# Second stage of a Fourier transform: two array tiles of 64 rows by 128 columns in place of four of 64 by 64

## The chip, the cores and the metric

The kernel runs on one core of a Trainium2 chip. The metric is the time on the device, in microseconds (us), of one execution: the median of three runs. Besides these, one execution was recorded by the hardware profiler; every duration below that is not called a median comes from that execution. TensorE (PE in the profile) has two levels of clock, 1.2 and 2.4 GHz; the profile calls them a granted clock of 0.5 and 1.0.

## The reference

The input is 8 sequences of 1856 rows with 256 features. A layer of a spectral kind comes first, and a mixture of experts after it:

```python
X = np.fft.rfft(x, axis=1)
Yr = Xr @ w_r - Xi @ w_i + b_r
Yi = Xr @ w_i + Xi @ w_r + b_i
Yr = np.sign(Yr) * np.maximum(np.abs(Yr) - lam, 0.0)     # Yi alike, lam = 0.01
y = np.fft.irfft(Yr + 1j * Yi, n=1856, axis=1)           # then 14848 rows of 256
g_idx = argmax(y @ w_group)                              # one of 4 groups
e_idx = argmax(y @ w_expert[g_idx])                      # one of 4 experts in it
out = g_w * e_w * (relu(y @ w1[g, e]) @ w2[g, e])        # 256 -> 1024 -> 256
```

## The kernel before

The sequences are worked on in four pairs (`pr`, two sequences `bt` in each). 1856 is 58 x 32, so the forward transform has two stages. The first (`a_mm`, line 349) sums over 58 rows with matmuls in four array tiles of 64 x 64; VectorE turns the result in blocks of 32 x 32 (line 353), which leaves, on 64 partitions for each half `h` of the 256 features, the 32 rows and the two parts (cosine, sine) that the second stage sums over. The second stage (`f_mm`, line 675) is the one that changes. For one frequency class (`k`, `kp`) and one sequence `bt` it multiplies the turned data, as the stationary operand, with a table `T` of 64 rows and 64 columns. The two halves `h` of the features lie on partitions 0 to 63 and 64 to 127, and so in different rows of the array; the 128 features of a half are cut again into two times 64 (`dh`), which lie in different columns of the array. Each matmul is of type float32 and leaves two loads of weights and two matmul records in the trace. One call of `f_mm`, a unit, fills the two banks of one PSUM tile with four frequency classes: 64 matmul records (32 where only half a tile is left). There are 30 full units' worth in all, 1920 records.

ScalarE and VectorE take the result out of PSUM (`f_high`, `f_low`, `d_copy`, `d_sub`, lines 692 to 707), and TensorE multiplies it with the complex weights (`m_common`, `m_mm`, lines 739, 742 and 757). The inverse transform has two stages as well (`b_mm`, line 782; `p_mm`, line 801). Its result goes to memory and through the router (`g_mm`, line 834; `route_g`), and GpSimd writes each row's number and weight into the list of its expert with indirect DMAs of 128 rows each (`scatter`, line 254; 128 of them in the kernel). The experts follow (lines 492, 565, 566 and others).

Steps of the four pairs, of the router, of the scatters and of the first expert jobs are interleaved by a string written out by hand (`ORDER`, lines 45 to 61), a letter for a step; `e` is one unit of `f_mm`. The instructions of TensorE, VectorE, ScalarE, SyncE and GpSimd keep the order of this string on their engine. Each scatter also waits for a matmul step that stands before it in the string (`pace`, lines 257 to 260), and for the third scatter before it.

Of the kernel before, what the change touches and what calls it, by code (L numbers as in the profile page):

```python
# [131 lines left out]
def spectral_moe(ctx: ExitStack, tc: tile.TileContext, x, wri, bri, wgate, w1, w2, cst, out):  # L132
    nc = tc.nc
# [178 lines left out]
    T = cf.tile([128, K1, 64], F32, name="T")  # L312
# [7 lines left out]
    def banks():  # L320
        return pa.tile([128, 2, 512], F32, name="bank")
# [15 lines left out]
    zys = {}  # L337
# [280 lines left out]
    def steps_of(*dims):  # L618

        def wrap(fn):  # L620
            def run():
                for idx in np.ndindex(*[len(d) for d in dims]):
                    fn(*[d[i] for d, i in zip(dims, idx)])
                    yield
            return run()
        return wrap
# [38 lines left out]
    @steps_of(pairs, u8)  # L665
    def f_mm(pr, kk):
        psum["f", pr, kk] = unit = banks()
        for k in range(2 * kk, min(2 * kk + 2, 15)):
            c0 = k % 2 * 256
            for kp in range(2):  # L670
                for bt in range(2):
                    m = (2 * kp + bt) * 32
                    for dh in range(2):
                        for h in range(2):
                            nc.tensor.matmul(unit[64 * dh:64 * dh + 64, h, c0:c0 + 256].rearrange("p (j c) -> p j c", j=2)[:, :, m:m + 32],  # L675
                                             lhsT=zys[pr][64 * h:64 * h + 64, k, bt, 64 * dh:64 * dh + 64, kp],
                                             rhs=T[64 * h:64 * h + 64, 2 * k + kp, :], start=True, stop=True, skip_group_check=True)

    def side(ins, what, pr, kk, h):
        apart(ins, (what, pr, kk, h), *((o_, pr, kk, 1 - h) for o_ in ("hs" if what in "fc" else "fc")))  # L680
# [325 lines left out]
    def first_rows(_):  # L1006
# [5 lines left out]

    steps = dict(
        Q=weight_steps(), l=load_steps(), c=a_mm, d=a_turn, e=f_mm, f=f_high, h=f_low, i=d_copy, g=d_sub, j=m_bias, p=c_high, q=c_low, y=m_common, z=m_share, k=m_mm,
        m=m_relu, o=m_shrink, r=b_mm, s=b_turn,
        v=p_mm, w=p_out, x=p_turn,
# [291 lines left out]
    for i, (kind, q) in enumerate(jobs):  # L1308
# [5 lines left out]
        if i + 1 < len(jobs) and jobs[i + 1][0] == "r":  # L1314
            k, part = jobs[i + 1][1]
# [44 lines left out]
    with tc.For_i(KF, nfx, 1) as iv:  # L1360
# [9 lines left out]
        hts, h = [], hq.tile([128, 8, WIDE], F32, name="hh")  # L1370
# [43 lines left out]
```

## Time and profile before

| | |
|---|---|
| time, median of 3 runs (lowest to highest) | 1117.25 us (1115.56 to 1117.4) |
| time of the profiled execution | 1122.26 us |
| its span, from first to last instruction | 1120.5 us |
| mean granted clock of TensorE | 0.972 |
| TensorE matmul busy | 1052.7 us, 94% of the span |
| VectorE, ScalarE, GpSimd busy | 661.4, 488.2 and 429.6 us |
| matmuls of line 675 | 1920 records, 49.2 us busy, 20.7 us idle before them |

The transforms take about the first 345 us, with the first expert jobs starting inside the stretch that follows; the rest is the experts. Busy time of TensorE is the union of its records' durations, and a record lasts longer than it keeps its part of the array, so the busy share says little about how fast matmuls follow each other; for that one looks at how many records start in a stretch. "issue" as the cause of an idle time means that the engine waited for nothing that the profile shows.

### The profile page before, as it was taken

The numbers are of one execution on the slowest core, as the hardware profiler recorded it, in microseconds if no ns is written. First come the engines' busy times: TensorE is split into PE (matmuls) and PEld (weight loads), VectorE is DVE, ScalarE is ACT, GpSimd is POOL, SyncE is SP. The second block draws the span as 40 slices with busy tenths as digits, with TensorE's granted clock in tenths as the row PEclk, the third lists the DMA queues.
The fourth block names the chain that finished last, engine by engine and source line by source line (L and its number), as shares of the span: only waits on it lengthen the run. The fifth ranks groups of instructions, "written<-read, shape, count | busy, mean of one in ns | idle before, by whom it ended". The sixth has DMA issues, their size and how long they took to land.

```text
span 1120.5 us, 24142 instructions
## 1 busy us (share of the span) xinstructions
PE 1052.7 (94%) x9400; PEld 910.5 (81%) x9400; DVE 661.4 (59%) x1574; ACT 488.2 (44%) x1249; POOL 429.6 (38%) x519
## 2 busy tenths in 40 slices
PE   7999989889888888799999999999999999999996
PEld 4886767764665677688999999999999999999996
DVE  6879987664776766336636554536455456455532
ACT  2664545331542444223435553435445345444532
POOL 0120254443434466656234333334335343332422
PEclk9999999896998999899999999999999999999999
DMA  9504402320231453014223233313133133133110
GB/s 380 189 2 149 155 2 101 128 78 2 77 133 39 133 170 77 20 52 134 72 72 133 79 101 104 103 51 128 47 114 130 44 122 117 52 109 113 45 34 28
DMA packets 38886, 106.94 MB, mean 95 GB/s; under 512 B 17596, under 2 KB 19993, under 8 KB 32242
## 3 DMA queue, kind: packets, MB, share of 16 engines
q1 hardware_dynamic: 18130, 57.74, 15.4%
q0 software_dynamic: 15744, 30.71, 8.9%
q10 hardware_dynamic: 4896, 16.93, 3.9%
q8 instruction: 75, 1.23, 0.5%
q14 instruction: 41, 0.34, 0.1%
HBM read 71.26 MB, written 34.23 MB: 94 GB/s over the span
## 4 chain that ended last, share of the span: by engine, by line
PE 56%; issue 4%; DVE 1%; ACT 1%; another core or an unknown queue 1%; POOL 1%; DMA 0%; POOLq 0%; ACTq 0%; DVEq 0%
PE ph L492 24%; PE py L565 12%; PE py L566 6%; PE py L587 6%; PE pg L475 2%; PE ph L925 2%; PE bank L949 1%; PE bank L951 1%; PE py L600 1%; DMA lst<-ent,sloti 0%; PE bank L834 0%; DVE hl L937 0%; POOL out_dram L539 0%; POOL lst L254 0%
## 5 line engine op out<-in xcount | busy, mean ns | idle before, releaser
L492 PE MATMUL ph<-xth,big 128*128 128x256 f32 (+8 forms) x1280 | 290.9, 311 | 2.1 <-DVE rk_o L1146 1.2
L499 DVE SCALAR_TENSOR_TENSOR hl<-ph,hh 128x256 fp32r<-128x256 f32 (+8 forms) x528 | 168.7, 356 | 108.3 <-ACT hh L497 89.3
L492 PEld LDWEIGHTS ph<-xth,big 128*128 128x128 f32 x1280 | 216.5, 188 | 4.9 <-PE ph L492 1.9
L565 PE MATMUL py<-big,hh 128*128 128x512 f32 (+2 forms) x608 | 219.0, 400 | 0.0
L492 PE MATMUL ph<-xtl,big 128*128 128x256 f32 (+8 forms) x640 | 198.1, 310 | 0.3 <-DVE xtl L480 0.3
L497 ACT ACTIVATE hh<-ph 128x256 fp32r<-128x256 f32 (+8 forms) x528 | 153.0, 337 | 99.6 <-PE ph L492 84.9
L457 POOL DMA_INDIRECT xg<-ys_d,gi_r x92 | 90.3, 981 | 244.5 <-PE pg L475 222.7
L254 POOL DMA_INDIRECT lst<-ent,sloti x128 | 128.3, 1003 | 140.4 <-PE pw L757 42.0
L566 PE MATMUL py<-big,hl 128*128 128x256 f32 (+2 forms) x608 | 171.4, 282 | 0.2 <-DVE hl L499 0.2
L565 PEld LDWEIGHTS py<-big,hh 128*128 128x128 f32 (+2 forms) x608 | 113.0, 186 | 27.1 <-DVE yo L606 0.3
L539 POOL DMA_INDIRECT out_dram<-yo,si_r x92 | 92.0, 1000 | 93.3 <-issue 44.7
L492 PEld LDWEIGHTS ph<-xtl,big 128*128 128x128 f32 x640 | 120.3, 188 | 0.7 <-DVE xtl L480 0.5
L566 PEld LDWEIGHTS py<-big,hl 128*128 128x128 f32 (+2 forms) x608 | 113.2, 186 | 1.1 <-DVE hl L499 0.8
L571 DVE SCALAR_TENSOR_TENSOR yo<-py,ent_r,yo 128x256 f32<-128x256 f32 (+1 forms) x66 | 31.9, 484 | 135.2 <-ACT yo L570 119.9
L570 ACT ACTIVATE yo<-py,ent_r 128x256 f32<-128x256 f32 (+1 forms) x66 | 31.4, 475 | 150.6 <-PE py L566 93.7
L587 PE MATMUL py<-hh,big 128*128 128x320 f32 (+4 forms) x320 | 75.3, 315 | 0.0
L723 POOL TENSOR_TENSOR xdl<-xd,xdh 128x512 fp32r<-128x512 f32 (+1 forms) x23 | 28.1, 1223 | 118.3 <-ACT xdh L716 93.7
L757 PE MATMUL pw<-wh,xh 128*128 128x256 f32 x240 | 68.2, 305 | 4.5 <-DVE pw L747 2.3
L439 DVE TENSOR_TENSOR big<-xt,big 128x512 fp32r<-128x512 f32 x104 | 71.1, 684 | 1.0 <-ACT big L438 0.2
L675 PE MATMUL bank<-T,big 64*64 64x64 f32 x1920 | 49.2, 228 | 20.7 <-issue 18.0
L675 PEld LDWEIGHTS bank<-T,big 64*64 64x64 f32 x1920 | 40.5, 137 | 34.3 <-issue 24.6
L438 ACT CAST big<-xt 128x512 fp32r<-128x512 f32 x104 | 65.3, 628 | 0.0
(217 smaller groups left out, 1953.1 us busy)
## 6 DMA issues: line engine op xcount, KB each, us to landing
xt<-in_w_dram SPq DMA_DIRECT2D x34, 1024.0 KB
ys_d<-ysb ACTq DMA_DIRECT2D x32, 512.0 KB
big<-in_x_dram SPq DMA_DIRECT2D x8, 1024.0 KB
xt<-in_x_dram SPq DMA_DIRECT2D x8, 1024.0 KB
lst<-ent,sloti POOLq DMA_INDIRECT x128
lst<-L SPq DMA_DIRECT2D x1, 1920.0 KB
xg<-ys_d,gi_r POOLq DMA_INDIRECT x92
out_dram<-yo,si_r POOLq DMA_INDIRECT x92
```

Source lines behind the costliest of these rows:

```text
L254: ins = nc.gpsimd.indirect_dma_start(out=lst, out_offset=bass.IndirectOffsetOnAxis(ap=sl_, axis=0), in_=en_, in_offset=None, bounds_check= ...
L439: nc.vector.tensor_tensor(out=wt[:, 2 * i + 1, cs], in0=raws[i][:, cs], in1=wt[:, 2 * i, cs].bitcast(F32), op=ALU.subtract)
L457: ins = nc.gpsimd.indirect_dma_start(out=xg[0:m, c, :], out_offset=None, in_=ys_d[0:rows, :], in_offset=bass.IndirectOffsetOnAxis(ap=ids.g ...
L492: nc.tensor.matmul(o[:, :n], lhsT=a_[:, ch, fs], rhs=b_[:, ch, 0:n], start=k == 0, stop=k == 5)
L497: nc.scalar.activation(out=hh[:, f, cs], in_=o[:, cs], func=AF.Relu)
L499: nc.vector.scalar_tensor_tensor(out=hl[:, f, cs], in0=o[:, cs], scalar=0.0, in1=hh[:, f, cs].bitcast(F32), op0=ALU.max, op1=ALU.subtract)
L539: ins = nc.gpsimd.indirect_dma_start(out=out, out_offset=bass.IndirectOffsetOnAxis(ap=ids.si[0:ids.rows(t), t:t + 1], axis=0), in_=ysb, in ...
L565: nc.tensor.matmul(o, lhsT=hh[:, f, ts], rhs=w2b[:, :, f, :], start=f == 0, stop=f == 7, skip_group_check=True)
L566: nc.tensor.matmul(o[:, 0:D], lhsT=hl[:, f, ts], rhs=w2h[:, f, :], start=False, stop=f == 7, skip_group_check=True)
L587: nc.tensor.matmul(o, lhsT=w_[:, f, ds_], rhs=h_[:, f, 0:n], start=f == 0 and h_ is hh and w_ is w2h, stop=f == 7 and h_ is hh and w_ is n ...
L675: nc.tensor.matmul(unit[64 * dh:64 * dh + 64, h, c0:c0 + 256].rearrange("p (j c) -> p j c", j=2)[:, :, m:m + 32], lhsT=zys[pr][64 * h:64 * ...
L757: ins = nc.tensor.matmul(y, lhsT=a_[:, h, k % 2, j], rhs=t[:, j, h], start=False, stop=a_ is xl and h == 1, skip_group_check=True)
```

## The change

The loop over `dh` goes away. One matmul takes all 128 features of a half as its stationary operand, and writes all 128 partitions of the PSUM bank. The two halves `h` stay in different rows of the array, so there are two array tiles of 64 rows by 128 columns instead of four of 64 by 64. The moving operand, the sums, the places of the results and all other steps are as they were.

```diff
                     m = (2 * kp + bt) * 32
-                    for dh in range(2):
-                        for h in range(2):
-                            nc.tensor.matmul(unit[64 * dh:64 * dh + 64, h, c0:c0 + 256].rearrange("p (j c) -> p j c", j=2)[:, :, m:m + 32],
-                                             lhsT=zys[pr][64 * h:64 * h + 64, k, bt, 64 * dh:64 * dh + 64, kp],
-                                             rhs=T[64 * h:64 * h + 64, 2 * k + kp, :], start=True, stop=True, skip_group_check=True)
+                    for h in range(2):
+                        nc.tensor.matmul(unit[:, h, c0:c0 + 256].rearrange("p (j c) -> p j c", j=2)[:, :, m:m + 32],
+                                         lhsT=zys[pr][64 * h:64 * h + 64, k, bt, :, kp],
+                                         rhs=T[64 * h:64 * h + 64, 2 * k + kp, :], start=True, stop=True, skip_group_check=True)
```

On TensorE, at the unit of the second stage that starts at 43.06 us in the trace of before, stands this (`pw` is the product with the complex weights, `bank` a PSUM tile; the last number is how many alike follow each other, and each float32 matmul of line 675 leaves two records):

```order
L757 MATMUL pw<-wl,xh 128x256
L757 MATMUL pw<-wh,xl 128x256 x2
L675 MATMUL bank<-T,big 64x2x32 x32
L349 MATMUL bank<-big,cA 64x512 x4
L739 MATMUL pw<-wch,xdh 128x256
L739 MATMUL pw<-wcl,xdh 128x256
```

And in the changed kernel, where all lines behind the edit have a number that is lower by one:

```order
L756 MATMUL pw<-wl,xh 128x256
L756 MATMUL pw<-wh,xl 128x256 x2
L674 MATMUL bank<-T,big 128x2x32 x16
L349 MATMUL bank<-big,cA 64x512 x4
L738 MATMUL pw<-wch,xdh 128x256
L738 MATMUL pw<-wcl,xdh 128x256
```

The unit keeps its place; it has 16 matmuls on 128 output partitions for 32 on 64. At the unit that starts at 162.85 us, behind a step of the inverse transform (line 782) of the pair before, the same engine has in the kernel before:

```order
L757 MATMUL pw<-wh,xl 128x256 x2
L782 MATMUL bank<-big,CI 64x512 x16
L675 MATMUL bank<-T,big 64x2x32 x32
L739 MATMUL pw<-wch,xdh 128x256
L739 MATMUL pw<-wcl,xdh 128x256
```

And in the changed kernel:

```order
L756 MATMUL pw<-wh,xl 128x256 x2
L781 MATMUL bank<-big,CI 64x512 x16
L674 MATMUL bank<-T,big 128x2x32 x16
L738 MATMUL pw<-wch,xdh 128x256
L738 MATMUL pw<-wcl,xdh 128x256
```

Here too nothing has moved but the count and the shape. The same holds for all 28 places of the line, and the rows of the other four engines are the same in both kernels but for line numbers.

## Rows read from the trace of the kernel before

**Rows 1.** Page, busy time: us, share of the span, instructions.

```profile
PE 1052.7 (94%) x9400; PEld 910.5 (81%) x9400; DVE 661.4 (59%) x1574; ACT 488.2 (44%) x1249; POOL 429.6 (38%) x519
```

**Rows 2.** Windows: length, busy us of each engine (instructions), granted clock, DMA share, GB/s.

```profile
30.00:150.00 120.00, 115.84 (x1899) 91.54 (x1892) 104.97 (x216) 69.26 (x151) 23.54 (x22) 1.00 0.33 109
150.00:345.00 195.00, 170.94 (x2159) 124.36 (x2158) 132.58 (x284) 79.06 (x173) 85.97 (x91) 0.88 0.23 75
```

**Rows 3.** Waits of TensorE, 150 to 345 us: total us, times, longest.

```profile
PE bank L675 <- issue: 16.1, 35, 1.1
```

**Rows 4.** Windows, line 675 alone, each unit of 30 to 150 us: length, PE, PEld.

```profile
35.69:36.67 0.98, 0.98 (x64) 0.98 (x64) 1.00 1.18 359
...
sum 13.59, PE 13.57 PEld 13.58; mean PE 1.04 PEld 1.04
```

**Rows 5.** Windows, line 675 alone, each unit from 150 us on.

```profile
162.85:167.61 4.76, 2.44 (x64) 1.90 (x64) 0.94 0.03 4
177.40:178.32 0.92, 0.92 (x64) 0.92 (x60) 1.00 0.00 0
...
sum 42.15, PE 25.53 PEld 20.26; mean PE 1.82 PEld 1.45
```

**Rows 6.** Timeline of TensorE, 12 to 24 us: start, us, what, records, idle before.

```profile
18.08 0.35 PE L675 MATMUL bank<-T,big 64*64 64x64 f32 x8 [1.41 <-DVE big L353]
18.68 2.02 PE L675 MATMUL bank<-T,big 64*64 64x64 f32 x117 [0.24 <-DVE big L353]
22.55 1.13 PE L675 MATMUL bank<-T,big 64*64 64x64 f32 x60 [1.85 <-issue]
```

**Rows 7.** Line 675, then line 742: duration ns min/median/max, first and last start.

```profile
L675 PEld LDWEIGHTS bank<-T,big x1920: 132/135/226, 16.3 to 333.5; 64*64 64x64 f32 x192
L675 PE MATMUL bank<-T,big x1920: 212/220/367, 16.3 to 333.5; 64*64 64x64 f32 x192
L742 PEld LDWEIGHTS pw<-wc,xd x68: 186/190/337, 24.5 to 347.5; 128*128 128x128 f32 x68
L742 PE MATMUL pw<-wc,xd x68: 378/379/794, 24.5 to 347.8; 128*128 128x256 f32 x68
```

**Rows 8.** Line 223: loads of bfloat16 weights.

```profile
L223 PEld LDWEIGHTS <-ones x8: 95/97/101, 129.8 to 437.6; 128*128 128x128 bf16 x8
```

**Rows 9.** Timeline of TensorE, 162 to 172 us.

```profile
162.85 1.26 PE L675 MATMUL bank<-T,big 64*64 64x64 f32 x43 [0.56 <-DVE big L790]
164.49 0.36 PE L675 MATMUL bank<-T,big 64*64 64x64 f32 x5 [0.39 <-issue]
165.22 0.35 PE L675 MATMUL bank<-T,big 64*64 64x64 f32 x5 [0.37 <-issue]
...
168.22 0.41 PE L739 MATMUL pw<-wcl,xdh 128*128 128x256 f32 x1
168.43 0.41 PE L739 MATMUL pw<-wch,xdh 128*128 128x256 f32 x1
```

**Rows 10.** Timeline of GpSimd, 160 to 169 us.

```profile
163.06 0.97 POOL L254 DMA_INDIRECT lst<-ent,sloti  x1 [0.30 <-issue]
```

**Rows 11.** Timeline of TensorE, 310 to 315 us.

```profile
312.15 0.40 PE L675 MATMUL bank<-T,big 64*64 64x64 f32 x12
313.14 1.08 PE L675 MATMUL bank<-T,big 64*64 64x64 f32 x52 [0.59 <-issue]
```

**Rows 12.** Windows of TensorE alone: length, busy (records), granted clock.

```profile
167.00:170.40 3.40, 3.00 (x18) 0.50 0.01 0
248.90:262.60 13.70, 13.32 (x71) 0.50 0.02 2
...
sum 34.10, PE 32.25; mean PE 5.38
```

**Rows 13.** Waits of GpSimd, 150 to 340 us.

```profile
POOL lst L254 <- PE pw L757: 39.0, 8, 14.0
```

**Rows 14.** Timeline of GpSimd, 300 to 480 us.

```profile
414.40 1.02 POOL L254 DMA_INDIRECT lst<-ent,sloti  x1 [5.48 <-DVE sloti L241]
```

## The prediction

> **What bounds the kernel now.** I read the page first, then windows of all engines, then the waits of TensorE, then line 675 by itself, unit by unit. TensorE is the busiest engine by far, 94% of the span against 59% for the next [rows 1]. The changed line lies in the first 335 us, so I looked there. From 30 to 150 us TensorE is busy for 115.8 of 120 us at the full clock. From 150 to 345 us it is busy for only 170.9 of 195 us, at a mean granted clock of 0.88, while no other engine passes 132.6 us [rows 2]. What makes it idle there is mostly not another engine: 16.1 us, in 35 pieces, stand directly before line 675 with "issue" as their cause [rows 3]. So TensorE bounds both stretches, and in the second one something holds it up at the very line that changes.
>
> The units show it. The 13 rows of units between 30 and 150 us (11 of 64 records, two of 96, so 14 units) take 13.59 us, 0.97 us a unit, without a break [rows 4]. The 14 rows from 150 us on (12 of 64, two of 32, so 13 units) take 42.15 us where 13 x 0.97 = 12.6 us would do [rows 5]: 29.5 us are stalls. They are uneven: one unit takes 0.92 us, another 4.76 us. In the slow one 43 records run in the first 1.26 us, then 5 records come every 0.7 us, and the engine waits for nothing in between [rows 9]. GpSimd is issuing scatters 0.30 us behind each other at that moment [rows 10]. This is so everywhere: the ten unit rows that lie beside such indirect DMAs are those that break, and the 17 others after the first block never do. I take this as the mechanism: while GpSimd issues indirect DMAs, instructions reach TensorE slowly (some ten in 0.7 us), and line 675, whose records start 15 ns apart, uses up what is queued. Nothing in the trace says why they come slowly.
>
> Six of the breaks are followed by a slow clock: six stretches of 34.1 us in all, between 167 and 303.5 us, run at 0.50, each beginning inside or right behind a broken unit [rows 12]. There line 739 starts a record every 0.21 us [rows 9].
>
> The stalls are not made by the profiler: the profiled execution took 1122.26 us, only 5.0 us over the median of 1117.25 us, and stalls and slow clock together are far more. I work out the sum in the profiled execution and carry it to the median as it is.
>
> **The change part by part.** Removed are 960 matmuls and 960 loads; added is width: each remaining load has 128 columns for 64. TensorE's order is otherwise the same and so is every other engine's, so no DMA, wait or queue is passed.
>
> *Longer loads.* Now four tiles share 64 records in 0.97 us, so each tile takes 16 loads, one every 61 ns. After, two tiles share 32 records: again 16 loads in each. A 64-column float32 load lasts 135 ns, a 128-column one 190 ns, and at its shortest 132 and 186: 54 ns more [rows 7]. The load sets the pace if the tile's own matmul is hidden under it; a record of line 742 with 256 columns lasts 379 ns, one of line 675 with 64 lasts 220 ns, so 64 columns keep the tile for about 53 ns (159 ns / 3, an estimate), and 61 ns a pair leaves no room for load and matmul one after the other. So a unit grows by 16 x 54 ns = 0.85 us, to 1.82 us. Bounds: nothing (a tile's pace stays at 61 ns), or twice the time if the two tiles took turns, which the present four do not. I take 0.85 us. Before 150 us: 14 x 0.85 = +11.9 us, with nothing to hide it (TensorE idles 4.2 us of 120, in waits that follow its own order). From 150 us on: 13 x 0.85 = +11.0 us.
>
> *The first block,* three units from 16.33 to 23.5 us, waits 1.41 and 0.24 us for VectorE, which stays, and 1.85 us for "issue" after 117 records [rows 6]. 3 x 0.85 = 2.55 us more, and I take the 1.85 us as gone, with half the instructions: +0.7 us; +2.5 us if not.
>
> *Stalls.* Nine of the ten units that break do so after 26 to 43 records, the tenth after 12 [rows 9, 11]. A unit will have 32, and last long enough (1.82 us) for some 12 more to arrive. So nearly every unit should be through on what is queued. The lines behind start from an emptier queue, so I leave 6 of the 29.5 us: -23.5 us. Bounds: 0 and -29.5 us.
>
> *Clock.* The stretches at 0.50 hold 3.7 us of the broken units themselves; the other 30.4 us would take at best half, -15.2 us. Some of that is work that waits for instructions or DVE at either clock (71 records in 13.7 us is less than the clock explains), so I take two thirds: -10 us. Bounds: 0 and -15.2 us.
>
> Sum: +0.7 + 11.9 + 11.0 - 23.5 - 10 = -9.9 us, 1122.3 to 1112.4 us in the profile, 1117.25 to about 1107 us in the median. With all bounds at their best end but the loads as taken, -21 us: 1096 us.
>
> What is late next: GpSimd. It waits for TensorE for 39.0 us in this stretch at one line alone [rows 13], so it has room to come earlier; a scatter's own place still follows TensorE's steps.
>
> **Two rules weighed.** Line 223 loads 128 columns of bfloat16 in 97 ns, line 742 as many of float32 in 190 ns, and neither has column tiles [rows 7, 8]. The Trainium skill (TensorEngine Tiling (Array Packing), Restrictions and Gotchas) says that column tiling shuts out a fast way of loading weights, which would speak for dropping it; another of its pages (TensorE: Matmul & The Clock Gate, Weight-path perf modes) says that float32 has no such way. The two durations agree with the second page, so the first rule should bring nothing; if it did, the loads would cost nothing, which is the third rival's sum.
>
> The Trainium skill (TensorE: Matmul & The Clock Gate, The mechanism) says that a load overlaps a running matmul only in other rows of the array. By it a tile of the changed kernel would do load and matmul one after the other, the second rival's case. The 61 ns a pair of today, less than a load and a matmul together,, speak against it for loads of 64 columns; no run here shows it for 128.
>
> **Rivals.**
> 1. *Slower: the breaks follow time, not count.* If scatters hold up the instructions from their own start, whatever is queued, a unit of 32 breaks as one of 64 did. For it: one unit broke after 12 records and 0.2 us [rows 11]. Against: 26 to 43 in the others, and units beside no scatter never break. Then the 9.5 broken units stay as long as now, the clock stays, the 1.85 us stay, and the other units pay: 2.5 + 11.9 + 3.5 x 0.85 = +17.4 us, 1135 us. It decides if fewer than about 16 records get through before the first break. Chance 0.18.
> 2. *Slower: load and matmul in turn.* A pair takes 61 + 54 + 53 = 168 ns in place of 115, so 30 x 16 x 53 ns = 25.4 us more than the forecast: 1133 us. Chance 0.06.
> 3. *Faster: the wide load costs nothing.* 30 x 0.85 = 25.5 us less: about 1082 us. No float32 row is that short. Chance 0.06.
> 4. *No change: given back later.* From 414 us GpSimd issues scatters almost without a gap, and what TensorE gained might only lengthen the wait for them. Against: that run of scatters begins after a wait of 5.48 us for the router on VectorE [rows 14], which hangs on TensorE's own steps and would come earlier with them. 1117 us, two to either side. Chance 0.10.
>
> **How the numbers follow.** The forecast has 0.60, with its own range of 1096 to 1115 us. Rivals 1, 2 and 3 lie outside it. From 1090 to 1135 us leaves out rival 3 (0.06) and about half of rival 1 with a little of rival 2, some 0.13. A difference of 0.2%, 2.2 us, is about what a measurement of this kernel can tell from none. Faster by more: the forecast less a little (0.58) and rival 3, 0.64. Within: most of rival 4 and the forecast's upper edge, 0.12. Slower: rivals 1 and 2, 0.24.
>
> **What the changed profile would show.** Units of line 674 before 150 us of about 1.8 us with 32 records, and no break; 1.0 us would show rival 3, 2.7 us rival 2. From 150 us on a sum over the 14 rows of about 30 us (24 without any break) against 42.15; over 40 is rival 1. "issue" before the line down from 16 us to a few. A granted clock from 150 to 345 us of 0.95 or more for 0.88; if the clock stays at 0.88, the term of -10 us is wrong. If all three are as said and the end does not move, it is rival 4, and the gap must stand between 345 and 480 us.

## Result: slower by 0.6%, and the profile after

The changed kernel takes 1124.35 us (median of 20 runs, 1118.72 to 1128.91), the kernel before in the same rounds 1116.42 us (20 runs, 1109.59 to 1123.22). The ratio is 1.0062, with a 95% interval of 1.0044 to 1.0081. The forecast was 1107 us, with a range of its own from 1096 to 1115 us: the kernel was to become some 10 us faster, and by the medians it became 7.9 us slower.

The profiled execution of the changed kernel took 1119.59 us, with a span of 1117.8 us. That is 2.7 us *less* than the span of before. The profiled execution of before (1122.26 us) would lie near the top of its runs, the one of after lies near the bottom of its own. So the two traces can say what each stretch does, but not which kernel is faster; for that the timed runs stand.

The page's busy times, and the two stretches by windows, answer to [rows 1, 2]; the last row is a window of TensorE alone, in the first block (length, busy, records, granted clock):

```profile
PE 1067.2 (95%) x8440; PEld 925.8 (83%) x8440; DVE 662.9 (59%) x1574; ACT 488.1 (44%) x1249; POOL 429.3 (38%) x519
```

```profile
30.00:150.00 120.00, 118.42 (x1324) 93.73 (x1324) 95.88 (x187) 62.18 (x131) 16.75 (x15) 1.00 0.33 108
150.00:345.00 195.00, 181.76 (x1932) 137.25 (x1932) 150.26 (x332) 90.22 (x199) 95.28 (x101) 0.99 0.23 75
```

```profile
20.10:30.30 10.20, 10.20 (x84) 0.50 1.00 414
```

The mean clock from 150 to 345 us is now 0.99 for 0.88. But from 20.1 us, inside the first units of the changed line, TensorE runs at 0.50 for 10.2 us, while its records lie end to end. Before, that stretch was at full clock.

The units of line 674, one row each (length, PE, PEld, clock): the last three before 163.5 us with the sum of those 13 rows, against [rows 4], and some of the 14 later rows with their sum, against [rows 5]:

```profile
147.44:149.28 1.84, 1.84 (x32) 1.84 (x32) 1.00 0.00 0
154.12:156.89 2.77, 2.77 (x48) 2.77 (x48) 1.00 0.00 0
161.63:163.46 1.83, 1.83 (x32) 1.83 (x32) 1.00 0.01 1
sum 25.72, PE 25.71 PEld 25.71; mean PE 1.98 PEld 1.98
...
178.98:180.82 1.84, 1.84 (x32) 1.84 (x32) 1.00 0.02 1
190.99:192.82 1.83, 1.83 (x32) 1.83 (x32) 1.00 0.15 63
208.23:210.06 1.83, 1.83 (x32) 1.83 (x32) 1.00 0.74 287
...
242.40:243.29 0.89, 0.89 (x16) 0.89 (x16) 1.00 0.12 37
...
331.03:331.92 0.89, 0.89 (x16) 0.89 (x16) 1.00 0.03 1
sum 23.77, PE 23.76 PEld 23.76; mean PE 1.70 PEld 1.70
```

Every full unit takes 1.83 us, where 1.82 was forecast, and none breaks: 13.59 us have become 25.72, and 42.15 have become 23.77. The loads and matmuls of the line, against [rows 7] (ns, min/median/max):

```profile
L674 PEld LDWEIGHTS bank<-T,big x960: 189/193/329, 18.1 to 331.9; 64*128 64x128 f32 x192
L674 PE MATMUL bank<-T,big x960: 277/278/419, 18.1 to 331.9; 64*128 64x64 f32 x192
```

A load lasts 193 ns for 135. From one record of a tile to its next pass 118 ns, for 60 before: 58 ns more, as much as a load lasts longer, and not the 168 ns that rival 2 gave for load and matmul in turn. So load and matmul overlap in one tile here too, and the rule that the prediction put beside rival 2, that a load overlaps a matmul only in other rows, does not hold for these loads. The Trainium skill (TensorE: Matmul & The Clock Gate, LDWEIGHTS (loading the stationary operand)) puts a load at its number of columns divided by 1.2, in ns: for 128 columns some 107 ns, an estimate from that formula, and the pace of 118 ns in the trace is near it.

What TensorE waits for from 150 to 345 us, against [rows 3] (us in total, times, longest):

```profile
PE pw L756 <- DVE pw L746: 4.1, 7, 1.5
PE pw L756 <- issue: 3.3, 3, 2.0
PE bank L781 <- issue: 1.3, 3, 0.8
PE bank L833 <- issue: 0.8, 1, 0.8
```

The 16.1 us of "issue" before the changed line are gone. A little of it stands at other lines now. All that the prediction wanted to see in this trace is there: 1.8 us a unit, no break, a sum of 24 us, "issue" gone, the clock at 0.99. Still the timed runs are not faster. So the question is where the gain went.

TensorE from 254 to 264 us in the changed kernel shows it (start, us, records, idle before):

```profile
255.30 2.10 PE L674 MATMUL bank<-T,big 64*128 64x64 f32 x32
257.33 1.13 PE L741 MATMUL pw<-wc,xd 128*128 128x256 f32 x4
258.39 3.07 PE L781 MATMUL bank<-big,CI 32*64 32x512 f32 x30
261.61 0.62 PE L781 MATMUL bank<-big,CI 32*64 32x512 f32 x1 [0.15 <-issue]
263.01 0.58 PE L781 MATMUL bank<-big,CI 32*64 32x512 f32 x1 [0.79 <-issue]
263.53 0.39 PE L756 MATMUL pw<-wh,xh 128*128 128x256 f32 x1
```

The unit passes whole. One step later, line 781 needs 4.62 us from its first record to its last, at full clock; the same 32 records at 90.52 us, before the first scatter, need 1.39 us. The shortage of instructions has not gone, it meets the next line. And it hardly shows as idle time: a record of line 781 lasts longer than the gap to the next, so TensorE counts as busy while it starves. The same could be read in the trace of before, where line 782 in the same place takes 6.33 us at half clock (5.27 us from first to last record):

```profile
252.19 6.33 PE L782 MATMUL bank<-big,CI 32*64 32x512 f32 x32
```

### The profile page after: what moved, and what is told of

Same layout as the page of the kernel before. It is cut to its first block, busy times and chain, and to the rows that moved or that the text cites. A ratio compares the mean times of both kernels' runs of the same rounds, so it can differ in the third digit from the quotient of the medians.

```text
span 1117.8 us, 22225 instructions
## 1 busy us (share of the span) xinstructions
PE 1067.2 (95%) x8440; PEld 925.8 (83%) x8440; DVE 662.9 (59%) x1574; ACT 488.1 (44%) x1249; POOL 429.3 (38%) x519
## 4 chain that ended last, share of the span: by engine, by line
PE 85%; issue 5%; DVE 5%; another core or an unknown queue 2%; ACT 2%; DMA 1%; POOL 1%; POOLq 0%; ACTq 0%; DVEq 0%
PE ph L492 24%; PE py L565 12%; PE pw L756 7%; PE py L566 6%; PE py L587 6%; PE bank L674 5%; PE ph L924 3%; PE bank L781 3%; PE pw L738 3%; PE bank L800 3%; PE pg L475 2%; PE bank L833 2%; PE bank L948 2%; PE bank L349 2%
## 5 line engine op out<-in xcount | busy, mean ns | idle before, releaser
L571 DVE SCALAR_TENSOR_TENSOR yo<-py,ent_r,yo 128x256 f32<-128x256 f32 (+1 forms) x66 | 31.9, 484 | 136.6 <-ACT yo L570 113.9
L674 PEld LDWEIGHTS bank<-T,big 64*128 64x128 f32 x960 | 62.1, 202 | 12.1 <-DVE big L353 3.0
L674 PE MATMUL bank<-T,big 64*128 64x64 f32 x960 | 66.2, 291 | 2.5 <-DVE big L353 1.8
```

Of the source, the lines that this page charges most:

```text
L674: nc.tensor.matmul(unit[:, h, c0:c0 + 256].rearrange("p (j c) -> p j c", j=2)[:, :, m:m + 32], lhsT=zys[pr][64 * h:64 * h + 64, k, bt, :, kp],
```

## The experiments

My account after this reading: the wide load costs some 0.8 us a unit everywhere and lets the clock fall in the first block; what it saves are the breaks of the changed line alone; and both breaks and the slow lines around them come from the scatters. The rivals: that the breaks shown in the one profile of before are rarer in its other runs; that wide units are slow for a reason outside these stretches; that the scatters have no part in it. "Late" below means the 13 units from [rows 5], from the third unit of the third pair on, and the stretch from their first to their last record.

**Both kernels again, and the change in halves.** `narrow_again` and `wide_again` are the kernels before and after. `late` has the wide matmul in the late units only, and `early` in the others (the condition of the diff with < for >=). All four ran on one chip, where before takes 1123.53 us.

```diff
+                    if (pr, kk) >= (2, 2):
+                        for h in range(2):
+                            nc.tensor.matmul(unit[:, h, c0:c0 + 256] ...
+                        continue
                     for dh in range(2):
                         for h in range(2):
```

> The kernel before, unchanged, for a second trace of it. Theory 1 (the first trace caught an execution with more and longer breaks than usual): time within 0.3% of the kernel before, but the 14 unit rows from 150 us on sum to clearly less than 42.15 us (30 to 36 us), and TensorE's mean clock is above 0.972. Theory 2 (the breaks are as usual, and what their removal gains is given back after 345 us): the sum is again 40 to 44 us and the clock 0.97 to 0.975.

Measured: ratio 1.0003 [0.9981, 1.0025]; its trace has 42.5 us in the late units against 42.0 in before (first to last record of each), and nine of its rows break. The breaks are no accident of one profile.

> The changed kernel, unchanged, for a second trace of it. Both theories: ratio 1.004 to 1.008 to the kernel before, units of 1.82 us without a break. Theory 3 (the first three units, now bound by loads, let the clock fall, 20 to 30 us in the first trace of the changed kernel): the clock is again at 0.5 for 7 to 14 us from about 20 us on. If that was chance: 1.0 throughout the first 100 us.

Measured: 1127.47 us, ratio 1.0049 [1.0022, 1.0076]. The slow clock in the first block is there again, for 13.7 us from 18.8 us on. And one wide unit does break, beside GpSimd's first gathers for the experts (line 457, indirect DMAs like the scatters):

```profile
313.96 1.70 PE L674 MATMUL bank<-T,big 64*128 64x64 f32 x23
316.69 0.72 PE L674 MATMUL bank<-T,big 64*128 64x64 f32 x9 [1.03 <-issue]
```

It is the unit that in before starts at 312.15 us and breaks after 12 records; there too gathers of line 457 stand beside it and no scatter, though the prediction counted it among the ten beside scatters.

> Wide tiles only in the 13 units from the third unit of the third pair on (162.85 us in the trace of before), narrow ones in the first 17. If the first trace of before is typical and nothing is given back: the 16.4 us that the changed kernel made up between these places in its trace, so ratio 0.985. Theory 1: about half of that or less, 0.992 to 0.998. Theory 2: 0.999 to 1.001.

Measured: 1113.26 us, ratio 0.990 [0.9865, 0.9934]: this half alone is faster than the kernel before, by 11.2 us by its ratio, and faster than the whole change. Its trace, held against that of `narrow_again`, has 17.6 us less in the late units (24.9 for 42.5) and 6.3 us more in the lines between them (132.9 for 126.6): 11.3 us less together. The same wide unit breaks as in `wide_again`. The 0.985 that was expected if nothing is given back lies below the interval.

> Wide tiles only in the first 17 units, narrow ones in the last 13, where scatters run. Longer loads alone: +11.9 and +0.7 us, ratio 1.011. Theory 3: 3 to 4 us more for the clock of the first block, so +16 us, 1.014, and early times late gives the ratio of the whole change, 1.006, within 0.3%.

Measured: 1140.28 us, ratio 1.0165 [1.0126, 1.0204]: 18.5 us slower by its ratio, 16.8 by the medians. The 1.014 that was expected with the slow clock of the first block lies in the interval, the 1.011 of longer loads alone does not. The product of the two ratios is 1.0063, the whole change. In early's trace the late stretch begins at 178.83 us for 164.49 in `narrow_again`, 14.3 us later, and then takes 174.97 us for 169.08: in this one trace another 6 us are lost among units that are as before.

**Without the first block.** `not_first` has the wide matmul everywhere but in the first three units (the condition is `(pr, kk) >= (0, 3)`).

> The changed kernel with narrow tiles in the first three units alone. Theory 3 (in the first block the load-bound units let the clock fall, which costs 3 to 4 us beyond the longer loads): the third-pair unit that lies at 179 to 180 us in the traces of the changed kernel comes at 175 us (4 to 5 us earlier), the first 40 us are at the full clock but for 3.4 us at most, ratio to the kernel before 1.001 to 1.003. If the first block cost only its longer loads (2.55 us): 1.003 to 1.005.

Measured: 1116.5 us against 1117.57 before, ratio 0.9997 [0.9968, 1.0026]. Compared with the whole change, 1.0062, 1.0049 and 1.0074 in three measurements (the last two on other chips, that of the first is not on record), the three units are worth 0.5 to 0.8%, 6 to 9 us, each uncertain by some 4 us. Its first block (20 to 25 us, by windows: PE, PEld, DVE, ACT, POOL, clock) has a clock of 0.81 with 158 records, where the changed kernel has 52 records at 0.51 in the same five us:

```profile
20.00:25.00 5.00, 4.79 (x158) 3.78 (x151) 4.68 (x9) 3.74 (x8) 0.00 (x0) 0.81 1.00 413
```

**Only beside the scatters.** `beside` has the wide matmul only in the ten units that broke; `beside_e` is the same on another chip.

```diff
+                    if (pr, kk) in ((2, 2), (2, 4), (2, 5), (2, 6), (3, 1), (3, 2), (3, 3), (3, 4), (3, 5), (3, 7)):
```

> Wide tiles only in the ten units that broke in the trace of before, those beside scatters. Against wide in all of the last 13 units (0.990): 3.5 units x 0.85 us less load time, so 0.986 to 0.988, if the units that did not break stay unbroken. If the narrow units among them now break, because places have moved: 0.990 or more.

Measured: 1106.05 us, ratio 0.9886 [0.9852, 0.9921].

> Wide matmuls only in the ten units that broke. Where before takes about 1,118 us: 0.989 times as long, as measured once. Where before takes about 1,055 us: slower, by nine and a half units of 0.85 us each, 8 us or 1.008 times as long; if it were still faster there, the wide unit would help by something other than the breaks.

Measured: 1110.37 us against 1124.27, ratio 0.9895 [0.9864, 0.9925]. The result holds on a second chip; it beats both kernels, and can't be told from `late`. Part of what the units gain is lost between them here too: in the two traces the late units take 23.0 and 22.4 us, for 42.0 in before, but the other lines of the late stretch 136.4 and 136.6 us, for 128.5 in before and 126.6 in `narrow_again`. The unit beside the gathers breaks in both.

**Without scatters.** `ns_narrow` and `ns_wide` leave out all 128 scatters (the lists of the experts then stay unfilled, so the experts' gathers read row 0 and their stores are skipped).

```diff
             sl_, en_ = pend.pop(0)
+            continue
             ins = nc.gpsimd.indirect_dma_start(out=lst, ...
```

> The kernel before without its 128 scatters (the index lists stay as zeroed, so the experts' gathers read row 0 and their stores are skipped). Theory 4 (instructions reach TensorE slowly while GpSimd issues indirect DMAs, and that is what breaks the units): no unit of line 675 breaks but in the first block; the 14 rows from the third pair on sum to 12.6 us in place of 42; and the other lines between them, 124 to 126 us with scatters whether the tiles are narrow or wide, drop below 110 us, because they too were short of instructions. If the breaks come from elsewhere: 35 us or more, and 124 us.

> The changed kernel without its 128 scatters, to be held against the kernel before without them (the same lists of zeros). Theory 4: there is nothing to win back, so the wide tiles cost their loads alone: 30 x 0.85 us and 3 to 5 us of the first block, 28 to 31 us more than the narrow tiles without scatters, ratio between the two 1.025 to 1.028. If the scatters were not the cause: 7 us more, 1.006.

Measured: 1044.38 us, ratio to before 0.936 [0.9332, 0.9389], and 1072.34 us, ratio 0.9608 [0.9579, 0.9636]. Of the kernel's 1117.57 us, 73 hang on the scatters. They do not come from the experts' changed gathers and stores: from the first record of line 475 of before, where most of the expert work begins, to the end of the span pass 621.1 us in before and 621.4 in `ns_narrow`. The late stretch is 46.4 us shorter, the way from the last unit to that record 31.1 us (165.9 and 134.8). Without scatters the wide kernel is 28.0 us slower than the narrow one; in the two traces the fourth unit starts 6.7 us later, the way to the late units takes 10.9 us more and the late stretch 10.0 us more. The late stretch whole, in before, after, and both kernels without scatters (length, PE, PEld, DVE, ACT, POOL, clock):

```profile
162.85:333.54 170.69, 149.73 (x1988) 109.51 (x1988) 114.81 (x249) 70.16 (x151) 72.38 (x78) 0.89 0.26 85
```

```profile
178.98:331.92 152.94, 144.70 (x1572) 107.10 (x1572) 115.14 (x250) 70.07 (x151) 71.22 (x76) 0.99 0.29 95
```

```profile
161.84:286.11 124.27, 122.41 (x1996) 92.40 (x1988) 113.66 (x249) 69.84 (x151) 13.41 (x19) 1.00 0.34 116
```

```profile
179.42:313.65 134.23, 133.34 (x1580) 102.91 (x1572) 115.37 (x250) 69.74 (x151) 13.60 (x19) 1.00 0.32 107
```

Take the units off (42.15, 23.77, 13.8 and 23.6 us, first to last record): the other lines of the stretch take 128.5, 129.2, 110.5 and 110.6 us (below 110 was expected without scatters). They cost the same in before and after, at a clock of 0.89 and of 0.99 alike, and 18 us less only when the scatters are gone. This is the main finding: the scatters hold up TensorE at other lines than the changed one too, and these lines as a whole gained nothing from the clock that came back.

Line 782 shows it best, here in the late stretch of before, after and `narrow_c` (a trace without the disturbance, below): records, busy us and mean ns, idle us before them.

```profile
L782 PE MATMUL bank<-big,CI 32*64 32x512 f32 x160 | 17.7, 820 | 0.0
L781 PE MATMUL bank<-big,CI 32*64 32x512 f32 x160 | 15.6, 651 | 1.3 <-issue 1.3
L782 PE MATMUL bank<-big,CI 32*64 32x512 f32 x160 | 10.0, 600 | 0.0
```

At half clock it ran for 12.4 us in before and for 1.8 us in after, and yet busy and idle together came down only from 17.7 to 16.9 us, where 10.0 do without the disturbance. Not all lines are like it. Counted from the start of each record to the start of the next, lines 739, 742 and 834 (by the numbers of before) together went from 43.3 to 39.8 us, and lines 757, 801 and 349 from 64.1 to 68.5.

One late unit of `ns_narrow` still breaks (2.43 us at 224.31 us), which was not expected, and it too lies beside gathers for the experts. So it need not be a scatter: the breaks of the late units in before, `wide_again` and `ns_narrow` stand beside indirect DMAs of GpSimd of either kind.

**Single runs of both kernels.** `narrow_c` and `narrow_d` are the kernel before, `wide_c` and `wide_d` the changed one, one run each, to see how much the late stretch varies.

> The kernel before, a third trace. Open is why the traces of narrow and wide tiles end within 3.5 us of each other (the wide ones earlier) while the medians put the wide ones 5 to 8 us later. Theory 1b (both earlier traces of the narrow tiles were of slow executions): an execution nearer to the median has the stretch from the third pair's third unit to the last unit at 160 to 167 us, not 169 to 171. Theory 2b (that stretch is the same in every execution, and the difference comes after the last unit): 169 to 171 us again, and the rest, after the last unit, at 782 to 786 us.

> The kernel before, a fourth trace; the same numbers as for the third.

> The changed kernel, a third trace. Both theories: the first block ends 5 to 6 us later than with narrow tiles, with the clock at 0.5 for 10 to 14 us. Theory 1b: the stretch from the third pair's third unit to the last unit at 153 to 156 us as in both earlier traces. Theory 2b: the same, and the rest at 790 us or more.

> The changed kernel, a fourth trace; the same numbers as for the third.

Measured: 1055.29, 1060.17, 1080.98 and 1082.39 us, with the kernel before beside them at 1054.84. The first block came as expected (the fourth unit 5.2 to 5.6 us later, the clock at half for 10.2 and 13.7 us); nothing expected of the late stretch or the rest was near. On this chip the kernel before is some 60 to 70 us faster than on the other chips, and the change costs 25 us (1081.7 less 1056.8, the means of two and of three single runs). The late stretch of the two kernels there (columns as above):

```profile
162.02:285.09 123.07, 120.84 (x1988) 91.94 (x1988) 116.27 (x250) 69.93 (x151) 66.69 (x73) 1.00 0.38 118
```

```profile
178.62:312.32 133.70, 133.07 (x1572) 102.37 (x1572) 117.01 (x251) 69.97 (x151) 69.39 (x76) 1.00 0.36 108
```

It is the stretch of the kernels without scatters, to 1.2 us, and yet the scatters are there. GpSimd and TensorE in `narrow_c`:

```profile
228.72 0.98 POOL L254 DMA_INDIRECT lst<-ent,sloti  x1 [0.30 <-issue]
230.00 0.98 POOL L254 DMA_INDIRECT lst<-ent,sloti  x1 [0.30 <-issue]
```

```profile
226.96 1.19 PE L675 MATMUL bank<-T,big 64*64 64x64 f32 x64
228.07 1.13 PE L742 MATMUL pw<-wc,xd 128*128 128x256 f32 x4
229.14 1.97 PE L782 MATMUL bank<-big,CI 32*64 32x512 f32 x32
```

The scatters last as long and follow each other as closely as on the other chips, and line 782, here in 1.97 us (1.39 from first to last record), is not held up. So whether scatters hold up TensorE depends on the chip or on the occasion; the four traces here are free of it, and the fifth run, of before, took no longer. In the traces of `narrow_c` and `wide_c` the change can be read off term by term: the fourth unit starts 5.6 us later (35.53 and 41.17 us), the way from it to the late units takes 11.0 us more (126.5 and 137.5), the late stretch 10.6 us more, the rest 1.5 us less: 25.7 us, the whole difference of the spans (1053.5 and 1079.2).

**Half of the scatters.** `half` is the kernel before with every second scatter left out; `wide_e` is the changed kernel. On this chip, again another one, before takes 1124.27 us.

```diff
+            skip.append(0)
+            if len(skip) % 2 == 0:
+                continue
             ins = nc.gpsimd.indirect_dma_start(out=lst, ...
```

> The kernel before with every second scatter left out (64 of 128; the lists of the experts are then not filled, so only the time counts). If each scatter holds instructions up for its own time, half of the 73 us that all 128 cost on one chip goes: where before takes about 1,118 us, half takes about 1,081 us. If the scatters' pace behind matmul steps matters more than their number, it stays above 1,100 us. Where before takes about 1,055 us, scatters hold nothing up, and half takes 1,045 to 1,055 us.

Measured: 1069.57 us, ratio 0.9501 [0.9456, 0.9546]: 55 us less. Both of its numbers were missed. The half that was left out carried far more than half of the loss that all of them cost on the other chip: the late stretch takes 134.80 us at a clock of 0.99, its units 21.97 for 42.15, and the other lines 112.8 us (134.80 less 21.97), nearly what they take without any. I read it as a matter of how closely scatters follow each other, but made no run that changes the spacing alone.

> The changed kernel again. Where before takes about 1,118 us: 1.005 times as long (5 us more), as measured twice. Where before takes about 1,055 us: 1.024 times as long (25 us more), since no unit of before breaks there and nothing is given back.

Measured: 1132.25 us, ratio 1.0074 [1.0045, 1.0102], the third such result.

## Why the prediction was wrong, by its own steps

The terms, from the profiles of before and after; each ends where a unit of the changed line starts or ends:

| term | forecast, us | measured, us | from |
|---|---|---|---|
| first block | +0.7 | +5.4 | fourth unit at 35.69, then 41.09 us |
| longer loads before the late units | +11.9 | +10.7 | 127.16 and 137.89 from there to the first late unit |
| late units, loads and stalls | +11.0 - 23.5 = -12.5 | -18.4 | 42.15 and 23.77 |
| clock, in the other lines of the late stretch | -10 | +0.6 | 128.5 and 129.2 |
| rest | 0 | -1.1 | 787.0 and 785.9 to the end |
| sum | -9.9 | -2.7 | spans 1120.5 and 1117.8 |

- *Longer loads:* right. The units before 163.5 us are 12.1 us longer (25.72 for 13.59), 0.87 us a unit for 0.85; 10.7 us of it, 0.77 a unit, reach the way to the late units. Rivals 2 and 3 fall with it: a unit takes 1.83 us, not 2.7 and not 1.0. On the chip without disturbance the late stretch gives the same price, 10.6 us for 13 units.
- *Stalls:* right in kind, and even more went than forecast. Rival 1, breaks that follow time, falls: in the three traces of the changed kernel on disturbed chips one of 42 late rows breaks, that of `wide_again` (its late units take 24.98 us, still far from 40).
- *Clock:* **this is the step that failed.** The clock came back, as the prediction wanted it (0.99 for 0.88), and for the -10 us the lines between the units gave +0.6: 128.5 us before, 129.2 after, and 110.5 with no scatters. The prediction took two thirds of the most that the slow stretches could give, with line 739 and its record every 0.21 us as the witness [rows 9, 12] (0.12 us at full clock in `narrow_c`). That line was no witness for the others: lines 739, 742 and 834 did get faster, by 3.5 us, but the largest part of the slow stretches, 12.4 of some 30 us, lay on line 782, which was short of instructions and stayed so. And lines 757, 801 and 349 lost 4.4 us. The second pair of traces says the same: 739, 742 and 834 4.2 us faster in `wide_again` than in `narrow_again`, 782, 757, 801 and 349 together 6.8 us slower. The remark that "the lines behind start from an emptier queue" named the right mechanism, but got 6 us of the stalls of the changed line; the shortage passed on took all that the clock gave back. That these 4 to 7 us are shortage passed on is my reading of where they appear; no run changes the clock alone.
- *First block:* the second failure. "Half the instructions" did end the wait for issue, but the clock went to 0.50 for 10.2 us in the middle of the 96 records, a thing the prediction had not among its bounds. They take 9.60 us from first start to last end; at the 118 ns of the later units it would be some 6 us (an estimate, 48 x 118 ns). The fourth unit comes 5.4 and 4.6 us later in the two pairs of traces; `not_first` puts the price at 6 to 9 us.
- *Rival 4*, given back later, was near: a part of the gain is given back in the next lines of the same stretch. The prediction's own sign of it (all three as said, and the end does not move) nearly came true, with an end that moved by 2.7 us, and asked for a gap between 345 and 480 us. The traces neither show nor exclude it: up to the last unit the kernels take the same (333.5 and 333.6 us in before and `narrow_again`; 331.9, 334.4 and 334.3 in after, `wide_again` and `wide_e`), and from there to the first record of line 475 165.9 and 173.9 us against 165.8, 169.6 and 174.6.

The timed runs say the same by halves: `early`, forecast at +12.6 us, measured +18.5; `late`, forecast at -22.5, measured -11.2 us. These two misses, 5.9 and 11.3 us, are nearly the whole way from -9.9 to +7.9, and they lie where the first block and the clock term lie.

That the two first traces put the changed kernel 2.7 us ahead and the medians put it 7.9 us behind is the spread of single runs, some 10 to 14 us from the lowest to the highest on the disturbed chips. In the traces most of it lies in one stretch: `narrow_again` ends 8.5 us later than before, and 8.0 of them are the way from the last unit to the first record of line 475, where the last scatters run; from that record to the end all five traces named here take 620 to 622 us. Carrying the sum from one profile to the median was therefore a risk the range should have named: the profile of before was 5.0 us over its median, and the prediction passed over that.

The main miss could have been seen beforehand: in before, line 782, which the change does not touch, needs 5.27 us from first to last of its 32 records at 252.19 us, and 1.39 us at 83.41 us. Half a clock explains at most twice 1.39, 2.8 us (an estimate). A shortage that slows three lines is not taken away by needing less at one of them.

Open is what scatters and gathers do to the delivery of instructions, and why one chip is free of it. The scatters' durations on GpSimd do not differ (median 978 ns in before and in `narrow_c`), nor do the bytes or packets of the queues. The packets of 16384 bytes on the queue that the profile calls "instruction" show no sign of it either: from 160 to 345 us 1.26 us in the mean and 2.39 at most each in before, 1.41 and 2.21 in `narrow_c`.

## What to carry to other kernels

When an engine waits with "issue" as the cause, first compare the pace of *all* its lines inside and outside the disturbed stretches, records per us rather than busy time; here fewer instructions at one line helped that line, and the next ones stayed short. A slow clock that sits on a starved stretch is not worth half of its length: price it line by line, only where records follow each other as closely as that clock allows. And make such a change where the trouble is: wide matmuls in the ten units that broke gave 1.1%, the same matmuls everywhere cost 0.6%.

## What the runs showed that was not expected

- 128 indirect DMAs of 128 rows, each 0.98 us of GpSimd's time (median), cost 6.4% of the kernel on one chip (ratio 0.936 without them); with every second one left out, 1.4% is left of that (the ratio 0.9501 of `half` less 0.936, on two chips).
- The same kernel took 1118 to 1124 us on three chips and 1055 to 1060 us in three single runs on a fourth, with the same scatters beside the same lines.
- TensorE's clock fell to 0.50 in a stretch in which its records lay end to end (20.1 to 30.3 us, wide loads with 64 moving columns, 10.20 of 10.20 us busy); in all seven traces with wide units in the first block it was at half clock there for 10.2 or 13.7 us, in the ten with narrow ones for 0 to 6.8 us. Single wide units of 1.83 us later on kept 1.00 in after.
